# One core, retention then a gated FFN: the first blocks of w3 by rows instead of by columns, two weight casts exchanged, one product in other PSUM banks

## The chip, the cores and the metric

The kernel runs on one core of a Trainium2 chip. The metric is the device time of one execution in microseconds (us). Before the change it is 186.15 us, the median of 13 runs (185.81 to 189.73).

The engines are named as the profile names them: PE (TensorE: matmuls and transposes, with PEld its weight loads), DVE (VectorE), ACT (ScalarE), POOL (GpSimd) and SP (SyncE, which here issues nearly all DMAs). Each engine executes its own instructions strictly in the order in which they stand in the program; engines wait for each other and for DMAs by semaphores.

## What is computed

```
# retention, 4 batches x 8 heads x 768 steps x 64
state = gamma[h] * state + outer(k[t], v[t])
y[t]  = q[t] @ state / sqrt(64)
x = y, heads side by side                       # [3072, 512]
# gated FFN; w1, w2 [512, 1024], w3 [1024, 1024], w_out [1024, 512]
h   = ((x @ w1) * (x @ w2)) @ w3
out = h @ w_out
```

## The kernel before

Since nothing lies between `@ w3` and `@ w_out`, the kernel first forms the product W3O = w3 @ w_out (eight tiles of 128 x 512), and then needs only x @ w1, x @ w2, their product, and one matmul with W3O. Retention is done in chunks of 128 time steps. A step handles one chunk of two batches (256 tokens); there are 12 steps (`NSTEP`). All matmuls take 16-bit inputs, so each weight and each of q, k, v is loaded in 32 bits into a staging tile and cast by DVE, ACT or POOL.

The order of the instructions is written out by hand, so the order of the statements is the order on each engine.

**Loads.** All loads go through `dma_in` (L63) on SP's queue. At most eight are under way, since the ninth waits for the first to land, and so on. The first eight alternate: a quarter of the first half of w3 (`load_w3_columns`, four pieces of 1 KB per partition), then a quarter of w_out (`load_wo`, 4 KB per partition), four times. Then come the last four row blocks of w3 (`load_rows`, 4 KB per partition), q, k, v of the first two batches, w1, w2, and the data of the later steps.

**W3O, first half (row blocks f = 0 to 3).** w3 has to be transposed on PE before it can be the stationary operand. For each column quarter i the program casts it (`cast_w3`, on DVE), transposes it in 8 PE instructions (`w3_transpose_columns`), copies the result back (`w3_back`, L254, on DVE), casts the matching quarter of w_out (`cast_wo`, ACT and POOL), and adds 8 matmuls, two to each of four open accumulators (`w3_mm_columns`, L283). All four row blocks are complete only after the last quarter. `output_decays` (three DVE multiplications, L206, and three ACT exponentials, L210; a table of decay factors for later) stands between the first and the second quarter. `busy(8, n=208)`, eight matmuls of zeros whose result nobody reads, stands there too.

**W3O, second half (f = 4 to 7).** Here a whole row block is cast (on ACT), transposed in 8 instructions (`w3_transpose`), copied back, and multiplied by all of w_out in 8 matmuls (`w3_mm`, L296). The first chunk of attention (`b0`, `b1`: objects of class `Pairs`, batch 0 and batch 1) is woven into this: q and k casts, their transposes (L349), scores (L446), the product with v (L464), the states (L477, L488 to L494), and the state's contribution to the output (L501).

**Start of the FFN.** `by_rows` (L746) runs x @ w1, and later x @ w2, for step 0 one row block of the weight after another, as each arrives. Row block 1 of w1 is cast on POOL (L732); 0, 2 and 3 on ACT (`cast_w`, L226), in this order. On POOL the cast of batch 1's v (`b1.v_cast`, L432) and the second half of `b0.states()` (L494) stand ahead of it.

**Step 2.** `step2` runs the FFN of step 1 between the parts of attention step 2. `f1.ab(f)` takes one accumulator from the four rotating PSUM banks `psF`; DVE's multiplication L651 frees it. `kv(2)` (L551), the product of k and v, writes the two banks `X0` and `X1`, the same two that `scores` uses; `kv_back(0)` (L573) and `kv_back(1)` (L565) read them on DVE. Step 3 then begins with `inter(2)` (L599) and `scores(3)` (L400).

**Steps 5 to 12.** At the start of a step m the program calls `intra(m - 1)` (L531), then `inter(m - 1)` (L599), which adds to the same banks and waits for the former. The wait goes through a mark: a 1 x 1 copy on ACT (`ended`, L587). For the m in `EARLY = (6, 11)` `intra(m - 1)` is instead called in the middle of the step before, and there is no mark.

Of the kernel before, what the change touches and what calls it, by code (L numbers as in the profile page):

```python
# [10 lines left out]
HP = mybir.dt.float16  # L11
# [7 lines left out]
def kernel(  # L19
# [11 lines left out]
    nc = tc.nc  # L31
# [19 lines left out]
    att = ctx.enter_context(tc.tile_pool(name="att", bufs=2))  # L51
# [53 lines left out]
    def new_stage():  # L105
        return wstage.tile([128, 1024], FP, tag="wst", name="stg")

    def load_rows(src, i):
        t = new_stage()
        dma_in(t[:, :], src[i * 128 : (i + 1) * 128, :])  # L110
        return t

    def load_wo(i):
        t = new_stage()
        dma_in(
            t[:, :].rearrange("p (t n) -> p t n", t=2),
            moe_w_out[i * 256 : (i + 1) * 256, :].rearrange("(p t) n -> p t n", t=2),
        )
        return t

    def load_w3_columns(i):
        t = new_stage()
        dma_in(
            t[:, :].rearrange("p (f c) -> p f c", f=4),
            moe_w3[0:512, i * 256 : (i + 1) * 256].rearrange("(f p) c -> p f c", p=128),
        )
        return t

    w3c_st, wo_st = [], []
    for i in range(4):  # L130
        w3c_st.append(load_w3_columns(i))
        wo_st.append(load_wo(i))
    w3_st = {f: load_rows(moe_w3, f) for f in range(4, 8)}
    for e in range(2):
        load_q(e)
        k_in[e] = load_pairs(k, e, 0)
# [1 line left out]
    w1_st = [load_rows(moe_w1, d) for d in range(4)]  # L138
# [12 lines left out]
    ident16 = const.tile([128, 128], HP, name="ident16")  # L151
# [21 lines left out]
    for s in range(2):  # L173
        r = slice(s * L, (s + 1) * L)
# [24 lines left out]
    for h in range(H):  # L199
        p, r = h // 2, (h % 2) * 64  # L200
        nc.gpsimd.memset(GS[r : r + 64, p : p + 1], gam[h] ** C)

    def output_decays():
        for n, (s, swap) in enumerate(((0, 0), (1, 0), (1, 1))):
            x = fsb.tile([128, NP, L], FP, tag="pa", name="ys_x", bufs=8)
            nc.vector.tensor_tensor(  # L206
                x[:, :, :], if_f[:, s, :].unsqueeze(1).broadcast_to((128, NP, L)),
                LGP[:, swap, :].unsqueeze(2).broadcast_to((128, NP, L)), MULT,
            )
            nc.scalar.activation(YS[:, n, :, :], x[:, :, :], AF.Exp)  # L210
# [4 lines left out]
    W1 = [wpool.tile([128, DFF], HP, name=f"w1_{i}") for i in range(4)]  # L215
    W2 = [wpool.tile([128, DFF], HP, name=f"w2_{i}") for i in range(4)]
    WO = [wpool.tile([128, 2, DM], HP, name=f"wo_{i}") for i in range(4)]
    W3O = [wpool.tile([128, DM], HP, name=f"w3o_{i}") for i in range(8)]
    W3h = {}
    w3t = {}  # L220

    def cast_to(dst, src, on_dve):
        if on_dve:
            nc.vector.tensor_copy(dst, src)
        else:
            nc.scalar.copy(dst, src)  # L226

    def cast_wo(i):
        dst = WO[i][:, :, :].rearrange("p a n -> p (a n)")
        if i == 0:  # L230
            nc.scalar.copy(dst, wo_st[i][:, :])
        else:
            nc.scalar.copy(dst[:, 0:512], wo_st[i][:, 0:512])
            nc.gpsimd.tensor_copy(dst[:, 512:1024], wo_st[i][:, 512:1024])

    def cast_w3(key, st):
        t = att.tile([128, 1024], HP, tag="qT", name="w3h", bufs=5)
        if key == ("c", 0):
            nc.vector.tensor_copy(t[:, 0:512], st[:, 0:512])
            nc.scalar.copy(t[:, 512:1024], st[:, 512:1024])  # L240
        else:
            cast_to(t[:, :], st[:, :], key in (("c", 1), ("c", 2), ("c", 3)))
        W3h[key] = t

    def bank(tag, shape, dtype, name):
        return ps_at.tile(shape, dtype, tag=tag, name=name)

    def w3_bank(key, i):
        src = W3h.pop(key)
        return src, bank(("X0", "X1")[i % 2], [128, 1024], HP, "psW3")  # L250

    def w3_back(key, ps):
        t = att.tile([128, 1024], HP, tag="v16", name="w3t", bufs=3)
        nc.vector.tensor_copy(t[:, :], ps[:, :])  # L254
        w3t[key] = t

    def w3_transpose_columns(i):
        src, ps = w3_bank(("c", i), i)
        for f in range(4):
            for t in range(2):  # L260
                g, c0 = f * 2 + t, f * 256 + t
                nc.tensor.transpose(  # L262
                    ps[:, g * 128 : (g + 1) * 128], src[:, c0 : c0 + 255 : 2], ident16[:, :]
                )
        w3_back(("c", i), ps)

    def w3_transpose(f):
        src, ps = w3_bank(f, f)
        for g in range(8):
            c0 = (g // 2) * 256 + g % 2  # L270
            nc.tensor.transpose(
                ps[:, g * 128 : (g + 1) * 128], src[:, c0 : c0 + 255 : 2], ident16[:, :]
            )
        w3_back(f, ps)

    def w3_mm_columns(i, acc, between=None, at=3):
        t = w3t.pop(("c", i))
        for f in range(4):
            if f == at and between:
                between()  # L280
            for r in range(2):
                g = f * 2 + r
                nc.tensor.matmul(  # L283
                    acc[f], lhsT=t[:, g * 128 : (g + 1) * 128], rhs=WO[i][:, r, :],
                    start=(i == 0 and r == 0), stop=(i == 3 and r == 1),
                )
            if i == 3:
                cast_to(W3O[f][:, :], acc[f], f < 3)
# [125 lines left out]
    class Pairs:  # L414
# [261 lines left out]
    def busy(m, tag="Y0", n=512):  # L676
        if tag:
            ps = bank(tag, [128, 512], FP, "psZ")
        else:
            ps = ps_f.tile([128, 512], FP, tag="psF", name="psZ")  # L680
        for _ in range(m):
            nc.tensor.matmul(ps[:, 0:n], lhsT=Z[:, 0:128], rhs=Z[:, 0:n], start=True, stop=True)  # L682

    cast_w3(("c", 0), w3c_st[0])
    busy(8)
    acc = [ps_f.tile([128, DM], FP, tag="psF", name="psW")[:, :] for _ in range(4)]
    w3_transpose_columns(0)
    cast_wo(0)
    output_decays()
    busy(8, n=208)  # L690
    cast_w3(("c", 1), w3c_st[1])
    w3_mm_columns(0, acc)
    w3_transpose_columns(1)
    cast_wo(1)
    cast_w3(("c", 2), w3c_st[2])
    w3_mm_columns(1, acc, lambda: w3_transpose_columns(2))
    cast_wo(2)
    cast_w3(("c", 3), w3c_st[3])
    w3_mm_columns(2, acc, lambda: w3_transpose_columns(3))
    cast_wo(3)  # L700
    cast_w3(4, w3_st[4])
    cast_w3(5, w3_st[5])
    w3_mm_columns(3, acc)
    w3_transpose(4)
    w3_transpose(5)
    cast_w3(6, w3_st[6])
    cast_w3(7, w3_st[7])
# [15 lines left out]
    b0.intra()  # L723
    b0.kv()
    b0.outputs_back(0)
    b0.states()
    b1.v_cast((nc.gpsimd, nc.gpsimd))
    b1.k_transposes(None, False)
    b0.inter()
    b0.outputs_back(1)  # L730
    busy(1, None)
    nc.gpsimd.tensor_copy(W1[1][:, :], w1_st[1][:, :])  # L732
    for d in (0, 2, 3):
        cast_w(W1, w1_st, d, False)

    ffn = [Ffn(m) for m in range(NSTEP)]
# [16 lines left out]
    ps = four_banks()  # L753
# [25 lines left out]
    ps = four_banks()  # L779
# [24 lines left out]
    def step2():  # L804
        am_back = scores(2)
        am_back(0)
        am_back(1)
        f0.o_unit(1)
        k_cast(3, (nc.gpsimd, nc.scalar))
        for f in range(2, 5):  # L810
            f1.ab(f)
        intra(2)
        kv_back = kv(2)
        kv_back(0)
        f1.ab(5)
        f1.ab(6)
        k_transposes(3, None, (True, False))
        kv_back(1)
        v_cast(3, (nc.gpsimd, nc.gpsimd))
        f1.ab(7)  # L820

    EARLY = (6, 11)

    K_PE = (3, 6, 8)

    def step(m):

# [100 lines left out]
```

## Time and profile before

| what | value |
|---|---|
| median of 13 runs | 186.15 us |
| the profiled execution | 187.42 us |
| its span in the profile | 185.8 us |
| PE busy | 174.7 us, 94% of the span |
| DVE, ACT, POOL busy | 108.9, 82.4, 59.1 us |
| PE busy from 0 to 38 us | 31.98 us |
| PE busy from 38 to 60 us | 21.49 us |
| DMA rate, slices from 0 to 18.6 us | 198, 361, 383, 405 GB/s |

The span is the time from the first to the last record of one profiled execution; 1.6 us of that execution lie around it. A timeline line has the start in us, the duration, the engine, the program's line, the operation, output and input tiles with shapes, the number of merged instructions, and in brackets how long the engine had been idle before and what ended that. An engine's busy share counts matmuls to their modelled ends. PE's idle time lies mostly in the first 40 us, where weights and the first data arrive.

### The profile page before, as it was taken

The page shows a single profiled execution, that of the slowest core. Times are in us where ns is not written, and L with a number is a line of the kernel's source. Part 1 is how long each engine was busy: PE and PEld are TensorE (multiplying, and loading weights), DVE is VectorE, ACT ScalarE, POOL GpSimd, SP SyncE. Part 2 cuts the span into 40 slices and gives each one's busy share as a digit, 9 for nine tenths or more (in the row PEclk, how much of TensorE's full clock was granted, in tenths as well). Part 3 has the DMA queues.
Part 4 walks back from the last instruction along what each step waited for, and adds up shares of the span by engine and source line. Part 5 has one row for each costly group of instructions (what it writes and reads, how often), then busy time and mean ns, then how long its engine had stood idle before and what let it go on. Part 6 is the DMA issues. An engine that isn't in the chain of part 4 may idle for free.

```text
span 185.8 us, 6230 instructions
## 1 busy us (share of the span) xinstructions
PE 174.7 (94%) x2642; PEld 124.8 (67%) x2642; DVE 108.9 (59%) x204; ACT 82.4 (44%) x166; POOL 59.1 (32%) x107
## 2 busy tenths in 40 slices
PE   7879899799999899999999999999999999999992
PEld 2434555488756487685876968859778587684871
DVE  1546557770749567848558584495685856845330
ACT  3524846556741332643445436354364442441531
POOL 7421143744543951533304425016251060000000
PEclk9999999999999999999999999999999999999999
DMA  5999999999899998999989989999999960200203
GB/s 198 361 383 405 301 278 341 407 374 232 185 218 273 210 185 214 255 261 218 189 199 257 255 170 156 249 253 264 166 130 216 206 137 4 113 0 14 102 0 113
DMA packets 80010, 39.44 MB, mean 212 GB/s; under 512 B 56304, under 2 KB 74992, under 8 KB 79984
## 3 DMA queue, kind: packets, MB, share of 16 engines
q1 hardware_dynamic: 79552, 38.54, 83.2%
q8 instruction: 20, 0.33, 0.8%
q10 hardware_dynamic: 432, 0.52, 0.8%
q14 instruction: 6, 0.05, 0.1%
HBM read 29.36 MB, written 6.29 MB: 192 GB/s over the span
## 4 chain that ended last, share of the span: by engine, by line
PE 75%; DMA 9%; SPq 6%; POOL 2%; issue 2%; ACT 2%; DVE 1%; ACTq 0%; POOLq 0%; DVEq 0%
PE psF L636 39%; PE psO L661 23%; SPq L63 6%; DMA stg<-in_moe_w_out_dram 5%; DMA stg<-in_k_dram 4%; PE psF L746 3%; PE psY L531 2%; PE psA L400 2%; PE psG L636 2%; PE psK L551 2%; PE psY L599 2%; POOL v L432 1%; PE psTk L375 1%; POOL k L311 1%; ACT qT L226 1%
## 5 line engine op out<-in xcount | busy, mean ns | idle before, releaser
L636 PE MATMUL psF<-xt,w 128*128 128x256 f16 x672 | 76.7, 273 | 0.0
L636 PEld LDWEIGHTS <-w 128*128 128x128 f16 x704 | 68.3, 98 | 10.4
L651 DVE TENSOR_TENSOR ht<-pa,psF 128x256 f16<-128x256 f32 x88 | 36.8, 420 | 39.4 <-PE psF L636 21.3
L661 PE MATMUL psO<-w3o,ht 128*128 128x512 f16 (+2 forms) x200 | 43.9, 371 | 0.8 <-issue 0.8
L645 ACT COPY pa<-psF 128x256 f32<-128x256 f32 x80 | 29.7, 372 | 33.4 <-PE psF L636 33.3
L661 PEld LDWEIGHTS <-ht 128*128 128x128 f16 x200 | 18.5, 98 | 20.7 <-issue 1.1
L665 ACT ACTIVATE osb<-psO 128x512 f32<-128x512 f32 (+2 forms) x25 | 14.5, 580 | 35.1 <-PE psO L661 35.1
L566 POOL TENSOR_TENSOR t<-s,GS 128x512 f16<-128x512 f32 x8 | 8.3, 1040 | 50.0 <-DVE s L565 50.0
L614 DVE TENSOR_TENSOR xt<-psY,YS 64x512 f16<-64x512 f32 (+1 forms) x29 | 21.0, 726 | 5.0 <-PE psY L599 4.7
L331 POOL TENSOR_TENSOR v<-stg,VS 128x512 f16<-128x512 f32 x20 | 20.5, 1042 | 6.4 <-DMA stg<-in_v_dram 6.3
L311 POOL CAST q<-stg 128x1024 f16<-128x1024 f32 x11 | 11.4, 1039 | 17.1 <-DMA stg<-in_q_dram 16.3
L407 DVE TENSOR_TENSOR am<-psA,keep 128x512 f16<-128x512 f32 x20 | 12.8, 682 | 1.7 <-PE psA L400 1.7
L746 PE MATMUL psF<-xt,w 128*128 128x256 f16 x64 | 8.4, 274 | 1.4 <-POOL w L732 1.1
L283 PE MATMUL psW<-wo,w3t 128*128 128x512 f16 x32 | 7.9, 380 | 1.6 <-DVE w3t L254 1.5
L254 DVE COPY w3t<-psW 128x1024 f16<-128x1024 f16 x8 | 5.5, 690 | 5.8 <-PE psW L262 3.2
L324 ACT CAST k<-stg 128x1024 f16<-128x1024 f32 (+1 forms) x9 | 8.5, 944 | 0.0
L296 PE MATMUL psW<-wo,w3t 128*128 128x512 f16 x32 | 8.1, 380 | 0.0
L746 PEld LDWEIGHTS <-w 128*128 128x128 f16 x64 | 5.8, 98 | 2.9 <-POOL w L732 1.3
L573 DVE TENSOR_TENSOR t<-psK,t 128x512 f16<-128x512 f32 x9 | 6.2, 689 | 0.6 <-PE psK L551 0.5
L283 PEld LDWEIGHTS <-w3t 128*128 128x128 f16 x32 | 2.7, 98 | 5.3 <-DVE w3t L254 3.0
L451 DVE TENSOR_TENSOR am<-psA,keep_t 128x512 f16<-128x512 f32 x8 | 5.2, 686 | 1.7 <-PE psA L446 1.7
L682 PE MATMUL psZ<-zeros 128*128 128x512 f16 (+1 forms) x17 | 4.9, 439 | 1.3 <-DVE zeros L150 1.3
(90 smaller groups left out, 149.2 us busy)
## 6 DMA issues: line engine op xcount, KB each, us to landing
stg<-in_moe_w_dram SPq DMA_DIRECT2D x16, 512.0 KB, 8.9
stg<-in_q_dram SPq DMA_DIRECT2D x12, 512.0 KB, 6.2
out_dram<-osb SPq DMA_DIRECT2D x22, 256.0 KB, 3.5
stg<-in_k_dram SPq DMA_DIRECT2D x20, 256.0 KB, 5.5
stg<-in_v_dram SPq DMA_DIRECT2D x20, 256.0 KB, 5.5
stg<-in_moe_w_out_dram SPq DMA_DIRECT2D x4, 512.0 KB, 8.6
stg<-in_k_dram SPq DMA_DIRECT2D x2, 512.0 KB, 9.3
stg<-in_v_dram SPq DMA_DIRECT2D x2, 512.0 KB, 8.2
```

The lines of the kernel that those rows point to most:

```text
L63: nc.sync.dma_start(dst, src)
L283: nc.tensor.matmul(acc[f], lhsT=t[:, g * 128 : (g + 1) * 128], rhs=WO[i][:, r, :], start=(i == 0 and r == 0), stop=(i == 3 and r == 1),)
L311: (nc.scalar.copy if eng is nc.scalar else eng.tensor_copy)(dst[:, :].rearrange("i (t h d) -> i h t d", t=2, d=D), src[:, :].rearrange("i ...
L331: eng.tensor_tensor(v16[:, e, :].rearrange("j (h d) -> j h d", d=D), v32[:, e, :].rearrange("j (h d) -> j h d", d=D), VS[:, 2, :].unsqueez ...
L407: nc.vector.tensor_tensor(am[:, r, :, :], ps[r][:, :, :], keep[:, :].unsqueeze(1).broadcast_to((128, NP * 2, L)), MULT,)
L614: nc.vector.tensor_tensor(XT[m][to, :, s, :].rearrange("p (a e) (i t) -> p a e t i", e=2, t=2), psYs[m][s][fr, :, :].rearrange("p (a e) (t ...
L636: nc.tensor.matmul(ps[:, :], lhsT=W[d][:, f * 128 : (f + 1) * 128], rhs=self.x(d), start=(d == 0), stop=(d == 3),)
L645: nc.scalar.copy(self.pa[f][:, :], ps[:, :])
L651: nc.vector.tensor_tensor(self.HT[:, f, :], self.pa.pop(f)[:, :], ps[:, :], MULT)
L661: nc.tensor.matmul(psO[:, :], lhsT=self.HT[:, f, e * 128 : (e + 1) * 128], rhs=W3O[f][:, cs], start=(f == 0), stop=(f == 7),)
L665: nc.scalar.activation(osb[:, cs], psO[:, :], AF.Copy, scale=final_scale)
L746: nc.tensor.matmul(ps[f // 2][:, f % 2, :], lhsT=W[d][:, f * 128 : (f + 1) * 128], rhs=f0.x(d), start=(d == 0 and f % 2 == 0), stop=(d == ...
```

## The change

Five edits.

1. The first four w3 loads take whole row blocks (f = 0 to 3), in turns with w_out as before; no load is made by columns.
2. Consequently W3O's first half is computed in another order: as each row block and each quarter of w_out arrives, the parts that have become possible are multiplied (`w3_part(f, *parts)`, two matmuls for each part). `busy(8, n=208)` comes before the first part, and `output_decays` comes after the second transpose instead of after the first. The tile `w3t` of f < 3 is taken from the buffers of `k16`.
3. `b1.v_cast` moves ahead of `b0.states()`, and POOL casts row block 2 of w1 where it cast row block 1; ACT casts 0, 1 and 3.
4. `kv(2)` writes two of the rotating `psF` banks instead of `X0` and `X1`.
5. `EARLY` becomes `(6, 11, 12)`.

The number of instructions on PE, DVE and POOL stays the same (matmuls, transposes, casts); ACT has one less, a mark.

```diff
-    w3c_st, wo_st = [], []
+    w3_st, wo_st = [], []
     for i in range(4):
-        w3c_st.append(load_w3_columns(i))
+        w3_st.append(load_rows(moe_w3, i))
         wo_st.append(load_wo(i))
-    w3_st = {f: load_rows(moe_w3, f) for f in range(4, 8)}
+    for f in range(4, 8):
+        w3_st.append(load_rows(moe_w3, f))
...
+        w3t[f] = att.tile([128, 1024], HP, tag="k16" if f < 3 else "v16", name="w3t", bufs=3)
+        nc.vector.tensor_copy(w3t[f][:, :], ps[:, :])
+
+    def w3_part(f, *parts):
+        for i in parts:
             for r in range(2):
-                g = f * 2 + r
+                g = i * 2 + r
                 nc.tensor.matmul(
-                    acc[f], lhsT=t[:, g * 128 : (g + 1) * 128], rhs=WO[i][:, r, :],
-                    start=(i == 0 and r == 0), stop=(i == 3 and r == 1),
+                    acc[f], lhsT=w3t[f][:, g * 128 : (g + 1) * 128], rhs=WO[i][:, r, :],
+                    start=(g == 0), stop=(g == 7),
                 )
             if i == 3:
                 cast_to(W3O[f][:, :], acc[f], f < 3)
...
-    cast_w3(("c", 0), w3c_st[0])
+    cast_w3(0)
     busy(8)
     acc = [ps_f.tile([128, DM], FP, tag="psF", name="psW")[:, :] for _ in range(4)]
-    w3_transpose_columns(0)
+    w3_transpose(0)
     cast_wo(0)
+    busy(8, n=208)
+    w3_part(0, 0)
+    cast_w3(1)
+    w3_transpose(1)
     output_decays()
-    busy(8, n=208)
-    cast_w3(("c", 1), w3c_st[1])
-    w3_mm_columns(0, acc)
-    w3_transpose_columns(1)
     cast_wo(1)
-    cast_w3(("c", 2), w3c_st[2])
-    w3_mm_columns(1, acc, lambda: w3_transpose_columns(2))
+    w3_part(0, 1)
+    w3_part(1, 0, 1)
+    cast_w3(2)
+    w3_transpose(2)
     cast_wo(2)
-    cast_w3(("c", 3), w3c_st[3])
-    w3_mm_columns(2, acc, lambda: w3_transpose_columns(3))
+    w3_part(0, 2)
+    w3_part(1, 2)
+    w3_part(2, 0)
+    cast_w3(3)
+    w3_transpose(3)
+    w3_part(2, 1, 2)
     cast_wo(3)
-    cast_w3(4, w3_st[4])
-    cast_w3(5, w3_st[5])
-    w3_mm_columns(3, acc)
+    cast_w3(4)
+    cast_w3(5)
+    for f in range(3):
+        w3_part(f, 3)
+    w3_part(3, 0, 1)
     w3_transpose(4)
+    w3_part(3, 2, 3)
     w3_transpose(5)
...
     b0.outputs_back(0)
+    b1.v_cast((nc.gpsimd, nc.gpsimd))
     b0.states()
-    b1.v_cast((nc.gpsimd, nc.gpsimd))
...
-    nc.gpsimd.tensor_copy(W1[1][:, :], w1_st[1][:, :])
-    for d in (0, 2, 3):
+    nc.gpsimd.tensor_copy(W1[2][:, :], w1_st[2][:, :])
+    for d in (0, 1, 3):
         cast_w(W1, w1_st, d, False)
...
-        kv_back = kv(2)
+        kv_back = kv(2, True)
...
-    EARLY = (6, 11)
+    EARLY = (6, 11, 12)
```

More of the change, by code (lines that the diff above doesn't have):

```diff
@@ L119, in load_wo @@
         return t
[L121 to L127, printed above, removed]
-    w3c_st, wo_st = [], []
+    w3_st, wo_st = [], []
     for i in range(4):
-        w3c_st.append(load_w3_columns(i))
+        w3_st.append(load_rows(moe_w3, i))
         wo_st.append(load_wo(i))
-    w3_st = {f: load_rows(moe_w3, f) for f in range(4, 8)}
+    for f in range(4, 8):
+        w3_st.append(load_rows(moe_w3, f))
     for e in range(2):
@@ L234, in cast_wo, with cast_w3 @@
             nc.gpsimd.tensor_copy(dst[:, 512:1024], wo_st[i][:, 512:1024])
-    def cast_w3(key, st):
+    def cast_w3(f):
         t = att.tile([128, 1024], HP, tag="qT", name="w3h", bufs=5)
-        if key == ("c", 0):
+        st = w3_st[f]
+        if f == 0:
             nc.vector.tensor_copy(t[:, 0:512], st[:, 0:512])
@@ L241, in cast_w3 @@
         else:
-            cast_to(t[:, :], st[:, :], key in (("c", 1), ("c", 2), ("c", 3)))
-        W3h[key] = t
+            cast_to(t[:, :], st[:, :], f < 4)
+        W3h[f] = t
     def bank(tag, shape, dtype, name):
         return ps_at.tile(shape, dtype, tag=tag, name=name)
[L248 to L265, printed above, removed]
     def w3_transpose(f):
-        src, ps = w3_bank(f, f)
+        src, ps = W3h.pop(f), bank(("X0", "X1")[f % 2], [128, 1024], HP, "psW3")
         for g in range(8):
@@ L273, in w3_transpose @@
             )
[L274 to L280, printed above, removed]
+        w3t[f] = att.tile([128, 1024], HP, tag="k16" if f < 3 else "v16", name="w3t", bufs=3)
+        nc.vector.tensor_copy(w3t[f][:, :], ps[:, :])
+    def w3_part(f, *parts):
+        for i in parts:
             for r in range(2):
-                g = f * 2 + r
+                g = i * 2 + r
                 nc.tensor.matmul(
-                    acc[f], lhsT=t[:, g * 128 : (g + 1) * 128], rhs=WO[i][:, r, :],
-                    start=(i == 0 and r == 0), stop=(i == 3 and r == 1),
+                    acc[f], lhsT=w3t[f][:, g * 128 : (g + 1) * 128], rhs=WO[i][:, r, :],
+                    start=(g == 0), stop=(g == 7),
                 )
@@ L682, in busy @@
             nc.tensor.matmul(ps[:, 0:n], lhsT=Z[:, 0:128], rhs=Z[:, 0:n], start=True, stop=True)
-    cast_w3(("c", 0), w3c_st[0])
+    cast_w3(0)
     busy(8)
     acc = [ps_f.tile([128, DM], FP, tag="psF", name="psW")[:, :] for _ in range(4)]
-    w3_transpose_columns(0)
+    w3_transpose(0)
     cast_wo(0)
+    busy(8, n=208)
+    w3_part(0, 0)
+    cast_w3(1)
+    w3_transpose(1)
     output_decays()
-    busy(8, n=208)
-    cast_w3(("c", 1), w3c_st[1])
-    w3_mm_columns(0, acc)
-    w3_transpose_columns(1)
     cast_wo(1)
-    cast_w3(("c", 2), w3c_st[2])
-    w3_mm_columns(1, acc, lambda: w3_transpose_columns(2))
+    w3_part(0, 1)
+    w3_part(1, 0, 1)
+    cast_w3(2)
+    w3_transpose(2)
     cast_wo(2)
-    cast_w3(("c", 3), w3c_st[3])
-    w3_mm_columns(2, acc, lambda: w3_transpose_columns(3))
-    cast_wo(3)
-    cast_w3(4, w3_st[4])
-    cast_w3(5, w3_st[5])
-    w3_mm_columns(3, acc)
+    w3_part(0, 2)
[4 more added lines that the diff above has]
+    w3_part(2, 1, 2)
+    cast_wo(3)
+    cast_w3(4)
[3 more added lines that the diff above has]
+    w3_part(3, 0, 1)
     w3_transpose(4)
+    w3_part(3, 2, 3)
     w3_transpose(5)
-    cast_w3(6, w3_st[6])
-    cast_w3(7, w3_st[7])
+    cast_w3(6)
+    cast_w3(7)
     w3_mm(4, lambda: w3_transpose(6))()
```

## The prediction, made before the changed kernel ran

> **What bounds the kernel now.** First the page: the busy shares and the chain of work that ended last.
>
> ```profile
> PE 174.7 (94%) x2642; PEld 124.8 (67%) x2642; DVE 108.9 (59%) x204; ACT 82.4 (44%) x166; POOL 59.1 (32%) x107
> ...
> PE 75%; DMA 9%; SPq 6%; POOL 2%; issue 2%; ACT 2%; DVE 1%; ACTq 0%; POOLq 0%; DVEq 0%
> ```
>
> PE bounds the kernel, and its instructions stay the same in number and shape. So the change is worth what it does to PE's waits: before 40 us, in step 2 (56 to 63 us), and at step 12. I take the timeline at these places. First the start:
>
> ```profile
> 6.72 1.08 DVE L206 TENSOR_TENSOR ys_x<-if_f,LGP 128x256 f32<-128x256 f32 x3
> ...
> 7.17 1.08 ACT L210 ACTIVATE YS<-ys_x 128x256 f32<-128x256 f32 x3 [0.34 <-DVE ys_x L206]
> 8.73 0.69 DVE L224 CAST w3h<-stg 128x1024 f16<-128x1024 f32 x1 [0.93 <-DMA stg<-in_moe_w_dram]
> ...
> 10.03 0.62 ACT L233 CAST wo<-stg 128x512 f16<-128x512 f32 x1 [1.77 <-DMA stg<-in_moe_w_out_dram]
> ...
> 10.89 1.47 PE L283 MATMUL psW<-wo,w3t 128*128 128x512 f16 x6 [0.79 <-DVE w3t L254]
> ...
> 14.32 0.69 DVE L224 CAST w3h<-stg 128x1024 f16<-128x1024 f32 x1 [0.69 <-DMA stg<-in_moe_w_dram]
> ...
> 15.60 0.62 ACT L233 CAST wo<-stg 128x512 f16<-128x512 f32 x1 [2.16 <-DMA stg<-in_moe_w_out_dram]
> ...
> 24.25 0.61 PE L349 MATMUL psTq<-ident,q 128*128 128x128 f16 x8
> ```
>
> The decays (L206, L210) lie in a gap in which DVE and ACT wait for DMA anyway (0.93 and 1.77 us of idle are left behind them). The eight matmuls of the first quarter (6.88 to 8.6) lie before it too. From 20.75 to 31.8 PE hardly waits: what delays it at 24.25 delays everything up to batch 1's scores. The landings show the DMA: a column load after a w_out load costs 1.50 us (12.82 to 14.32), a row-wise one after a column load 1.28 (14.32 to 15.60).
>
> **Edits 1 and 2, the start.** I follow the chain through the new order. *Landings.* Four column loads become row loads, each 1.50 − 1.28 = 0.22 us quicker. The first cast starts at 4.27 instead of 4.47, that of the second w3 block (two such loads) at 8.33 instead of 8.73. Bounds: 8.73, if pieces of 1 KB cost nothing, and 6.9 (4.27 and two row loads of 1.3) if the odd step of 2.95 us from 5.78 to 8.73 were due to columns; it looks like a start-up lag, so I take 8.33.
>
> *The new wait.* DVE casts (0.69), PE transposes (0.62), DVE copies back (0.69), with 0.05 us between each: to 10.43. Now come the three decays on DVE, 1.08, and behind them ACT's three exponentials, which end 0.45 after the last decay (8.25 against 7.80 before): 11.96. In ACT's queue the cast of the second w_out quarter stands behind them; its data has long landed (9.6). It ends at 12.6, and PE's next product (part 0,1) starts at 12.66. Before, this matmul group started at 10.89, and eight matmuls of the group before it were done, where now there are two. Queued on PE behind it are all parts of blocks 0 to 3.
>
> *From there to the first q transpose* PE has 46 matmuls of 128x512 (30 for blocks 0 to 3, 16 for blocks 4 and 5) at 0.216 (1.90 for eight, less the 0.17 tail) and six sets of transposes at 0.45: 9.94 + 2.70 = 12.64. Waits in between: 0.10 for the copy-back of block 2; 0.26 for block 3's cast, which DVE can begin only after that copy; 0.6 for block 6's cast, as ACT first has to evict block 3 (L226, 0.58), whose last part now ends at 21.0, after the transposes of block 4. Sum 12.66 + 13.6 = 26.26, against 24.25: **+2.0 us**. With the landing at 8.73 it is +2.4.
>
> [...]
>
> **Edit 3, w1's casts.**
>
> ```profile
> 35.27 1.03 POOL L732 CAST w<-stg 128x1024 f16<-128x1024 f32 x1
> ...
> 36.37 1.05 PE L746 MATMUL psF<-xt,w 128*128 128x256 f16 x8 [1.11 <-POOL w L732]
> ```
>
> POOL casts w1's block 1 only after the v cast (33.28, 2.05 us), which stood behind L494, which waits for DVE (2.03 us): PE waits 1.11. After: batch 1's data land by about 31 us, so v is cast before L494; ACT casts blocks 0 and 1 back to back behind kT. With +2.0, block 0's matmuls start at 35.84, ACT has block 1 at 36.9, the second scores run at 36.82, and block 1's matmuls start at 37.1, not at 38.4. Then DVE's masking of these scores (1.29 for two halves from 37.27) ends at 38.56 and takes the wait's place: the second half of intra starts at 38.62, `kv` and then block 2's matmuls at 39.24, against 38.20. Left: **+1.04**, so this edit gives back 0.96. Block 2's cast on POOL (free at 35.3) ends at 36.4, block 3's on ACT at 37.95: both hidden. From here to 56 us the waits are on work of PE's own chain (data for step 2 land 1 to 3 us early), so +1.04 stays.
>
> **Edit 4, kv(2) in psF.**
>
> ```profile
> 58.79 0.44 PE L400 MATMUL psA<-qT,kT 64*64 64x64 f16 x30 [0.28 <-DVE s L565]
> ...
> 62.96 0.81 PE L661 MATMUL psO<-w3o,ht 128*128 128x512 f16 x3 [0.82 <-issue]
> ```
>
> The scores of step 3 no longer wait for `kv_back(1)` (0.28). But counting the rotation, `f1.ab(7)` gets the bank that `kv` filled second, and waits for the same `kv_back(1)`, ending at 58.73. Its four matmuls (0.45) and `inter(2)` (0.37), which ran before that point, now run after it: 0.82, plus 0.02 for the start. The outputs then begin 0.84 later than the 59.16 of before. Cover: the 0.82 us in which PE stood still before 62.96, a wait that no engine's record explains ("issue"). If its end is tied to a moment in PE's stream ahead of the edit, it swallows 0.82 of the 0.84; if to the position alone, nothing. Ends 0.02 and 0.84; I take **0.02**, since nothing in the queues of the other engines holds these three matmuls, so it seems to be a supply of instructions running alongside.
>
> **Edit 5.**
>
> ```profile
> 167.68 0.19 ACT L587 COPY mark<-zeros 1x1 f16<-1x1 f16 x1 [0.47 <-PE psY L531]
> ...
> 167.93 0.45 PE L599 MATMUL psY<-qT,t 64*64 64x64 f16 x32 [0.31 <-ACT mark L587]
> ```
>
> Intra (0.38) moves to 161.8 in step 11; the masked scores are ready at 160.87 and Y's banks at 158.95. The 0.31 us of waiting goes: **−0.30**.
>
> **Sum** against the profiled execution: A +2.0, B −0.96, C +0.02, D −0.30 = +0.76; span 185.8 → 186.55, the execution 187.42 → 188.2. That execution is 1.27 above the median, so against the median 186.15: **186.9 us**.
>
> **Rivals.**
> *PE falls back to half rate.* Eight 128x512 matmuls took 3.60 us at 1.26 and 1.90 at 16.48. After the change PE does next to nothing from 7.3 to 12.66, two sets of transposes apart at most. If it slows, one more such stretch costs 1.70, nothing gives it back, and the time is 188.6. Against it: after the idle stretch 8.61 to 10.89, with transposes in it, matmuls ran at full rate; but now it is 5.4 us. The granted clock reads 1.00 throughout, even at 1.26, so the clock column won't tell; durations will.
> [...]
> *Edit 4's wait isn't covered:* +0.82, 187.7. For it: the stall's cause isn't shown.
> *Faster: the load lag belongs to the column loads.* If the second w3 block is cast at 6.9 instead of 8.33, the whole chain to 24.25 moves with it by 1.43: the sum becomes 0.76 − 1.43 = −0.67, 185.5. The sum passes nought at a cast at 7.57, and the difference can be measured from 7.0 on. Against it: at 5.7 us 1.3 MB had moved, at 8.7 us 2.4 MB, while the landed loads are 1.05 and 1.57; the DMAs worked without a gap, part of them ran ahead, and the slowest one sets the landing, whatever the shape.
> *The rows land early but nothing follows*, as PE was never waiting: the landings alone are then hidden, and the time stays at 186.1 to 186.4. This needs the decays off the chain, which the order of ACT's queue excludes; small.
>
> **Chances.** Forecast (186.4 to 187.4) 0.40; uncovered wait 0.20; half rate 0.18; faster 0.15; flat 0.07. Range 185.6 to 188.7. A measurement tells 0.3%, 0.56 us, from no change: faster is below 185.6, slower above 186.7. The forecast's own spread puts a third of it below 186.7: slower 0.27 + 0.20 + 0.18 = 0.65; same 0.13 + 0.07 + some of the faster case = 0.22; faster 0.13.
>
> **What would show it.** ACT's cast of the second w_out quarter starts near 12.0 behind L210's line, with no DMA wait; the first q transpose at 26.3; by_rows block 1 without a POOL wait and block 2 about 1 us later than 38.20; `f1.ab(7)` waiting for DVE's `s`, and no 0.82 us standstill in step 3's outputs; no mark at step 12. I am wrong if the second w3 cast starts before 7.6, if matmuls after 12.66 take 0.43 us each, or if a standstill appears elsewhere.

## The result, and the profile after

The changed kernel takes 188.33 us, the median of 11 runs (187.62 to 189.25). The kernel before has a median of 186.41 us (48 runs). The ratio is 1.0102, with a 95% interval of 1.0078 to 1.0126: the change makes the kernel 1% slower. All ratios leave out the runs that are over 1.5% above the fastest of the same kernel. The profiled execution took 188.88 us, its span 186.8, so 2.08 us lie around the span where 1.62 did before.

The page of the changed kernel: busy time by engine, the granted clock in 40 slices of 4.67 us (in tenths), and the chain that ended last.

```profile
PE 176.6 (95%) x2642; PEld 126.4 (68%) x2642; DVE 108.6 (58%) x204; ACT 81.7 (44%) x165; POOL 59.1 (32%) x107
...
PEclk9957999999999999999999999999999999999999
...
PE 75%; ACT 2%; DVE 1%; issue 0%; ACTq 0%; DVEq 0%
```

PE does the same 2642 operations but is "busy" 1.9 us longer. The clock row says where: slices 3 and 4, from 9.3 to 18.7 us. The windows of the changed kernel give the same by stage (stretch, its length, PE's busy time, granted clock, DMA share, GB/s):

```profile
9.00:14.00 5.00, 2.26 (x13) 0.58 1.02 416
14.00:18.60 4.60, 4.60 (x29) 0.71 1.04 392
18.60:23.30 4.70, 4.70 (x36) 1.00 1.16 292
```

Finer windows of the same trace show 1.00 from 6 to 9.80 us, 0.50 from 9.80 to 16.63, and 1.00 behind it: 6.83 us at half rate.

The timeline of the changed kernel at the start, in the columns used before:

```profile
8.15 0.69 DVE L217 CAST w3h<-stg 128x1024 f16<-128x1024 f32 x1 [1.63 <-DMA stg<-in_moe_w_dram]
...
10.61 1.09 ACT L203 ACTIVATE YS<-ys_x 128x256 f32<-128x256 f32 x3 [4.12 <-DVE ys_x L199]
...
11.61 1.12 ACT L226 CAST wo<-stg 128x512 f16<-128x512 f32 x2
...
12.26 2.72 PE L257 MATMUL psW<-wo,w3t 128*128 128x512 f16 x6 [2.74 <-ACT wo L226]
...
14.77 1.06 PE L246 MATMUL psW<-ident,w3h 128*128 128x128 f16 x8
...
27.48 0.61 PE L323 MATMUL psTq<-ident,q 128*128 128x128 f16 x8
```

ACT waits 4.12 us for DVE's decays. Its cast of the second w_out quarter stands behind the exponentials and has no DMA wait any more, and PE waits for that cast. Six products then take 2.72 us (1.47 before), and eight transposes 1.06 instead of 0.62: half rate.

Later places in the changed kernel's timeline: `by_rows` blocks 0, 1 and 2; step 2's `f1.ab(7)`, the second half of step 3's scores and its outputs; intra in step 11, and inter of step 12:

```profile
37.07 1.05 PE L729 MATMUL psF<-xt,w 128*128 128x256 f16 x8 [0.21 <-ACT w L219]
...
38.42 1.05 PE L729 MATMUL psF<-xt,w 128*128 128x256 f16 x8
...
40.44 1.05 PE L729 MATMUL psF<-xt,w 128*128 128x256 f16 x8
...
59.81 0.60 PE L610 MATMUL psF<-xt,w 128*128 128x256 f16 x4
...
61.16 0.32 PE L374 MATMUL psA<-qT,kT 64*64 64x64 f16 x16 [0.25 <-ACT kT L219]
61.41 3.63 PE L635 MATMUL psO<-w3o,ht 128*128 128x512 f16 x16
...
163.36 0.44 PE L505 MATMUL psY<-am,v 64*64 64x64 f16 x32
...
169.08 0.45 PE L573 MATMUL psY<-qT,t 64*64 64x64 f16 x32
```

Two of these places in the kernel before, `by_rows` block 2 and the outputs of step 3:

```profile
38.20 1.05 PE L746 MATMUL psF<-xt,w 128*128 128x256 f16 x8
...
59.16 2.98 PE L661 MATMUL psO<-w3o,ht 128*128 128x512 f16 x13
```

Block 1 no longer waits for POOL, step 3's scores wait 0.25 for kT on ACT where they waited 0.28 for DVE's `s`, step 3's 16 outputs run without a standstill (a stop of PE in the middle of a group, with nothing in the profile that it waits for), and step 12 has no mark. How far the changed kernel is behind at each place:

| place | before | after | behind |
|---|---|---|---|
| product after the second w_out cast | 10.89 | 12.26 | 1.37 |
| first q transpose | 24.25 | 27.48 | 3.23 |
| `by_rows` block 2 | 38.20 | 40.44 | 2.24 |
| outputs of step 3 | 59.16 | 61.41 | 2.25 |
| the FFN products behind them | 63.61 | 64.88 | 1.27 |
| outputs behind step 12's start | 168.30 | 169.46 | 1.16 |
| span | 185.8 | 186.8 | 1.0 |

The start costs 3.23, edit 3 gives back 0.99, edit 4 nothing (0.01). A standstill of the kernel before, which the changed kernel doesn't have in this execution, gives 0.98. Between 64.88 and step 12 the gap rises to 1.43, and edit 5 gives back 0.27.

### The profile page after: what moved, and what is told of

It reads as the page before. It is cut to its first block, busy times and chain, and to the rows that moved or that the text cites. A ratio compares the mean times of both kernels' runs of the same rounds, so it can differ in the third digit from the quotient of the medians.

```text
span 186.8 us, 6225 instructions
## 1 busy us (share of the span) xinstructions
PE 176.6 (95%) x2642; PEld 126.4 (68%) x2642; DVE 108.6 (58%) x204; ACT 81.7 (44%) x165; POOL 59.1 (32%) x107
## 4 chain that ended last, share of the span: by engine, by line
PE 75%; ACT 2%; DVE 1%; issue 0%; ACTq 0%; DVEq 0%
PE psF L610 38%; PE psO L635 22%; PE psF L729 4%; PE psY L505 2%; PE psA L374 2%; PE psG L610 2%; PE psY L573 2%; PE psK L525 2%; PE psTk L349 1%; ACT qT L219 1%; ACT w L219 1%; ACT osb L639 0%; PE psY L438 0%; DVE ht L625 0%; ACT kT L219 0%
## 5 line engine op out<-in xcount | busy, mean ns | idle before, releaser
L257 PE MATMUL psW<-wo,w3t 128*128 128x512 f16 x32 | 9.5, 444 | 2.7 <-ACT wo L226 2.7
L246 PEld LDWEIGHTS <-w3h 128*128 128x128 f16 x64 | 4.7, 109 | 5.2 <-DVE w3h L217 2.1
L270 PE MATMUL psW<-wo,w3t 128*128 128x512 f16 x32 | 8.1, 380 | 0.0
L257 PEld LDWEIGHTS <-w3t 128*128 128x128 f16 x32 | 3.4, 110 | 6.4 <-issue 4.5
L246 PE MATMUL psW<-ident,w3h 128*128 128x128 f16 x64 | 5.8, 243 | 1.9 <-DVE w3h L217 1.6
L219 ACT CAST w3o<-psW 128x512 f16<-128x512 f32 x5 | 2.9, 585 | 8.7 <-PE psW L270 4.6
```

The source lines that it names most:

```text
L246: nc.tensor.transpose(ps[:, g * 128 : (g + 1) * 128], src[:, c0 : c0 + 255 : 2], ident16[:, :])
L257: nc.tensor.matmul(acc[f], lhsT=w3t[f][:, g * 128 : (g + 1) * 128], rhs=WO[i][:, r, :], start=(g == 0), stop=(g == 7),)
```

## The experiments

Each kernel was timed beside the kernel before on the same chip. Four questions are asked: what the decays' place and the clock each cost; what edits 3 to 5 give; what the standstill is; and why 0.45 us more lie outside the span.

**The kernel before, again** (`e1_before_again`), with no edit.

> The kernel before, unchanged, so that its spread and its standstill at 62 us can be seen in a second profile. If the 0.82 us standstill in the outputs of step 3 belongs to a place in PE's stream, it is there again, with about the same length; if it depends on how other traffic happens to fall, it may be gone, and the span then is near 185.0 instead of 185.8. Time 186.1 to 186.5.

Measured: 186.06 us median, spans 184.2 to 185.1. Its profiled execution has no standstill; the 16 outputs of step 3 and the FFN products behind them:

```profile
59.30 3.63 PE L661 MATMUL psO<-w3o,ht 128*128 128x512 f16 x16
62.76 1.91 PE L636 MATMUL psF<-xt,w 128*128 128x256 f16 x16
```

From the first output to the FFN products it is 3.46 us here and was 4.45 in the profiled execution before. The standstill (0.99 with its surroundings) is in one of the two profiles of the unchanged kernel and not in the other.

**The decays back at their old place** (`e2_decays_early`):

```diff
     cast_wo(0)
+    output_decays()
     busy(8, n=208)
...
     w3_transpose(1)
-    output_decays()
```

> The changed kernel, but output_decays stands again right behind the cast of the first w_out quarter. My theory (the late decays hold ACT's cast of the second w_out quarter, and the idle stretch that follows halves PE's rate): that cast starts near 9.6 with no wait for the exponentials, part (0,1) starts near 10.3 instead of 12.26, the matmuls take 0.216 and not 0.43, the first q transpose falls back from 27.5 to 24.2-24.6, and the time is 185.0 to 186.0, below both kernels. Rival (the order by rows is itself what costs, since ten matmuls instead of eight are left after the last w_out quarter, and a block's eviction stands before the casts of blocks 6 and 7 on ACT): the first q transpose gains under 1.5 us and the time stays above 187.

Measured: 185.81 us (185.42 to 186.55), ratio 0.9959 [0.9932, 0.9986]: the whole loss is gone. Its timeline:

```profile
9.52 0.62 ACT L226 CAST wo<-stg 128x512 f16<-128x512 f32 x1 [1.63 <-DMA stg<-in_moe_w_out_dram]
...
10.19 2.35 PE L257 MATMUL psW<-wo,w3t 128*128 128x512 f16 x6 [0.56 <-ACT wo L226]
...
24.95 0.61 PE L323 MATMUL psTq<-ident,q 128*128 128x128 f16 x8
```

ACT's cast waits for its DMA again, and PE has it two us sooner. The six products still run mostly at half rate here (2.35). In five of the ten runs the mean clock was 0.988 to 0.991 and the span 183.8 to 184.5; in the other five 0.997 to 1.0 and 183.4 to 183.6. So the order by rows, with two products ahead of the gap where the order by columns has eight, costs something of its own: with the decays early and the second w3 cast at the same time (8.26 and 8.28), the order by columns further down (`e5_rows_only`) has its first q transpose at 23.39, this run at 24.95.

**Only the decays moved, in the kernel before** (`e6_cols_late_decays`):

```diff
     cast_wo(0)
-    output_decays()
...
     w3_transpose_columns(1)
+    output_decays()
     cast_wo(1)
```

> The kernel before, with column loads and its own order, in which only the three decays move behind the transposes of the second w3 load, ahead of the second w_out cast: the place that the change gives them. Theory (the place of the decays alone makes the late start): ACT's second w_out cast at about 12.4 instead of 10.03, the next product at about 13.0 instead of 10.89; 24 matmuls and two sets of transposes from there bring the last product of the first four blocks to 17.8 instead of 16.48, so the first q transpose is at 25.5 if PE stays at full rate, at 26.8 to 27.3 if the matmuls after 13.0 take 0.43 us each; span +1.3 to +2.9. Rival (the order by rows makes it, not the decays): the first q transpose stays within 0.3 of 24.3.

Measured: 188.69 us (4 runs), ratio 1.0134 [1.0102, 1.0166]. With column loads and the old order, one moved call makes the same picture:

```profile
11.38 1.12 ACT L233 CAST wo<-stg 128x512 f16<-128x512 f32 x2
...
12.03 1.48 PE L283 MATMUL psW<-wo,w3t 128*128 128x512 f16 x6 [2.74 <-ACT wo L233]
13.32 1.04 PE L262 MATMUL psW<-ident,w3h 128*128 128x128 f16 x8
...
14.16 3.23 PE L283 MATMUL psW<-wo,w3t 128*128 128x512 f16 x8
...
26.16 0.61 PE L349 MATMUL psTq<-ident,q 128*128 128x128 f16 x8
```

The first q transpose is 1.9 later than before, between the two numbers expected, although the second w3 cast came 1.43 earlier here (7.30). The first six products are at full rate and the next eight, after transposes, are at half: the mean granted clock is 0.93 from 9.3 to 14 us and 0.70 from 14 to 18.6; at 0.50 that puts its fall at 13.3 us, when the six have run, and its return at 16.8 (an estimate). The rival (the row order makes the loss) falls as the main cause; its smaller share is named above.

**Filler in the gap** (`e3_warm`): eleven products of zeros ahead of the decays, so that PE isn't idle.

```diff
     w3_transpose(1)
+    busy(11)
     output_decays()
```

> The changed kernel with eleven matmuls of zeros (128x512) behind the second w3 transposes, inside the time in which PE waits for the second w_out quarter; the wait itself stays. It parts the two halves of the loss. If half rate is an effect of the idle stretch, the matmuls from 12.3 on take 0.216 each, the first q transpose falls from 27.5 to 26.1-26.4, the mean granted clock is 0.99 or more and the time is 187.0 to 187.6. If the low rate has another cause, matmuls still take 0.43 and the time stays at 188.3.

Measured: 190.7 us, four runs from 187.76 to 192.07, ratio (of the two shorter ones) 1.012 [0.9985, 1.0256], unclear, and not the 187.0 to 187.6 expected. Two of the four still had a mean clock of 0.989 and 0.990. The profiled run had 0.998, and its trace is clearer than its time; the first products behind the gap, the first q transpose, and two places in the outputs:

```profile
11.86 1.46 PE L257 MATMUL psW<-wo,w3t 128*128 128x512 f16 x6 [0.37 <-ACT wo L226]
...
25.48 0.61 PE L323 MATMUL psTq<-ident,q 128*128 128x128 f16 x8
...
61.85 3.18 PE L635 MATMUL psO<-w3o,ht 128*128 128x512 f16 x14 [1.84 <-issue]
...
137.89 1.46 PE L635 MATMUL psO<-w3o,ht 128*128 128x512 f16 x6 [1.39 <-issue]
```

The six products run at full rate, 1.46 us. From them to the first q transpose (25.48) it is 13.62 us, against 15.22 in the changed kernel: the half clock costs the profiled execution of the changed kernel 1.60. In six of that kernel's twelve runs the mean clock is 0.981 or 0.982 as there (spans 186.7 to 187.2), in the other six 0.989 to 0.991 (185.5 to 186.2); these lost some 1.1 us less. What the filler gave was lost again to two standstills. In the kernel before 3 of the 16 outputs were left at the standstill, here 14: eleven products more have been put ahead, and the standstill has moved eleven products forward in the outputs. Counted in PE's program, weight loads and products each as one, both stand at number 1472, and the second at 4032, 2560 further. So in these two profiles the place belongs to a position in PE's program and not to the work done there.

**Edits 1 and 2 alone** (`e8_start_only`): the changed kernel, with `v_cast`, the casts of w1, `kv(2)` and `EARLY` as before.

> The changed kernel with edits 3, 4 and 5 undone: edits 1 and 2 alone. Theory (the start costs all of it, the other edits give back 1.3): second w_out cast on ACT at 11.6, matmuls from 12.2 at 0.43 us each, first q transpose at 27.5, block 2 of by_rows at 41.3 to 41.6, span 187.7 to 188.4, time ratio 1.015 to 1.022. Rival (edit 4 costs something that the trace of the changed kernel hides): span below 187.5, ratio about 1.010.

Measured: 189.2 us (4 runs), ratio 1.0173 [1.0138, 1.0208]; the six products start at 11.66, the first q transpose at 26.43, as the second w3 cast came at 7.55 here. At a clock of 0.989 to 0.991 its spans are 186.8 to 187.2, those of the changed kernel 185.5 to 186.2: edits 3 to 5 give back some 1.1 us of the 1.26 read from the profiles. The span is below 187.5, as the rival had it, but from the early cast. Edit 4 hides no cost: from `by_rows` block 2 to the outputs of step 3 it is 20.96 us here without the edit, 20.97 in the changed kernel with it.

**Edits 3 to 5, and 3 and 5, in the kernel before** (`e4_before_345`, `e7_before_35`):

```diff
+    b1.v_cast((nc.gpsimd, nc.gpsimd))
     b0.states()
-    b1.v_cast((nc.gpsimd, nc.gpsimd))
...
-    nc.gpsimd.tensor_copy(W1[1][:, :], w1_st[1][:, :])
-    for d in (0, 2, 3):
+    nc.gpsimd.tensor_copy(W1[2][:, :], w1_st[2][:, :])
+    for d in (0, 1, 3):
...
-        kv_back = kv(2)
+        kv_back = kv(2, True)
...
-    EARLY = (6, 11)
+    EARLY = (6, 11, 12)
```

The line of `kv(2)` is changed in the first of the two only.

> The kernel before with only edits 3, 4 and 5: w1's casts exchanged with v ahead of the states, kv(2) in psF, EARLY with 12. By my steps edit 3 gives 0.9 to 1.0 where block 1 of w1 is waited for, edit 4 nothing (the profile after shows the scores of step 3 now waiting for kT on ACT by 0.25 instead of for s by 0.28), edit 5 0.3: together 1.2, so 184.9 to 185.2. Rival: w1's block 1 has not landed when ACT gets to it (it lands near 33.8 here), or the standstill of step 3 grows by what was gained ahead of it, as it shrank by 0.98 when PE came 2.2 us late; then the gain is 0.3 to 0.5, 185.7 to 186.1.

> The kernel before with edit 3 (the v cast ahead of L494, the casts of w1's blocks 1 and 2 exchanged) and edit 5 (an early intra at step 12), without the rest. Theory: block 1 of by_rows without a wait for POOL, block 2 at 37.1 to 37.3 instead of 38.2, no mark at step 12; span 1.25 to 1.3 shorter than the kernel before in runs without a standstill (182.8 to 183.8), time ratio 0.993. Rival (the standstills in PE's stream take the gain up): time ratio 0.997 to 1.0.

Measured: 186.5 us, ratio 0.9972 [0.9932, 1.0012], and 186.49 us, ratio 1.0004 [0.9975, 1.0032]. No gain that can be told from nothing, with spans from 183.4 to 186.3 and from 183.5 to 186.1. From block 2 to the outputs of step 3 it is 20.96 us with edit 4 and 20.97 without, 20.96 in the kernel before: edit 4 is worth nothing here either. The shortest spans are 0.5 to 0.7 below the shortest of the kernel before in the same sets of runs (184.0 and 184.1), not 1.25. The profile of the run with 3 and 5 shows one way in which the gain goes (cast of w1's block 0, then blocks 0 and 1 of `by_rows`):

```profile
33.94 1.04 ACT L226 CAST w<-stg 128x1024 f16<-128x1024 f32 x1 [0.70 <-DMA stg<-in_moe_w_dram]
...
35.04 1.57 PE L746 MATMUL psF<-xt,w 128*128 128x256 f16 x8 [1.01 <-DVE am L451]
...
37.14 1.85 PE L746 MATMUL psF<-xt,w 128*128 128x256 f16 x8
```

The first block of w1 landed at least 1.2 us later than in the profile before (cast at 32.74 there, without a DMA wait). PE waited 1.01 for it (the masking named as the releaser ends at about the same moment as the cast; in the kernel before, the block starts in the middle of it), and then the clock fell (0.80 from 33 to 37 us, 0.77 from 37 to 41): 1.57 and 1.85 us for eight products that otherwise take 1.05.

**Only the loads by rows** (`e5_rows_only`), with the order of the columns kept; the first four blocks of W3O are then made of other pieces.

```diff
-        w3c_st.append(load_w3_columns(i))
+        w3c_st.append(load_rows(moe_w3, i))
```

> The kernel before, in which only the first four loads of w3 fetch whole rows (blocks 0 to 3) instead of column strips; the order of the products stays that of the columns, so the first four blocks of W3O are made of the wrong pieces. Theory (the DMA side of edit 1 is a gain of 0.2 us per load): the second w3 cast starts at 8.2 to 8.4 instead of 8.73, the fourth one 0.8 us earlier than 14.32, the first q transpose at 23.5 to 23.7 instead of 24.25 to 24.39; span 183.3 to 184.3 without a standstill. Rival (the landings are set by bytes alone): casts and the first q transpose where they were, span 184.1 to 185. On the 0.45 us by which the changed kernel's time exceeds its span more than before: if the row loads cause it, time less span is about 2.05 here, otherwise 1.6 to 1.7.

Measured: 185.31 us, ratio 0.9974 [0.9946, 1.0002]. The second w3 cast comes at 8.28, the next ones at 10.87 and 13.43. That is 2.57 us for a pair of loads, where the run with edits 3 and 5 has 2.79 (8.64, 11.43, 14.22): 0.22 for each row load. The first q transpose is at 23.39. But block 0 of `by_rows` is no earlier (33.84 in the kernel before):

```profile
23.39 0.61 PE L349 MATMUL psTq<-ident,q 128*128 128x128 f16 x8
...
32.86 1.04 ACT L226 CAST w<-stg 128x1024 f16<-128x1024 f32 x1 [0.87 <-DMA stg<-in_moe_w_dram]
33.96 1.84 PE L746 MATMUL psF<-xt,w 128*128 128x256 f16 x8 [1.18 <-ACT w L226]
```

PE arrives early, waits 1.18 us for w1, and its clock falls at the end of this wait (0.63 from 33 to 37 us, which at 0.50 puts the fall at 34.0, an estimate; eight products take 1.84). In the nine runs at a clock of 0.998 or more the span is 183.1 to 185.6, in the one at 0.988 it is 185.2.

**Early decays, with block 3 of W3O evicted by DVE** (`e9_early_evict_dve`), on top of the run with the decays at their old place:

```diff
-                cast_to(W3O[f][:, :], acc[f], f < 3)
+                cast_to(W3O[f][:, :], acc[f], True)
```

> The changed kernel with the decays early (as in the run with the decays at their old place) and block 3 of W3O evicted by DVE instead of ACT, so that ACT's casts of blocks 6 and 7 don't stand behind it. Theory (the eviction in ACT's queue costs the 0.31 us at the transposes of block 6): that wait is gone, the first q transpose at 24.3 to 24.7 instead of 24.95, block 0 of by_rows up to 0.3 earlier than 34.55, span 183.1 to 183.7, time 185.3 to 185.7. Rival (DVE has no room: its eviction holds the copy-back of block 5): the first q transpose at 25.0 or later, time 185.8 or more.

Measured: 185.5 us (184.38 to 186.36), ratio 0.9939 [0.9909, 0.9969], the lowest ratio of the study, ahead of both kernels. The first q transpose is at 24.05, block 0 of `by_rows` at 33.75 and block 1 at 35.68; the cast ahead of the latter, at 34.58, waits 0.89 us for its DMA. It is ahead of the profile without this edit by 0.90 at the q transpose, 0.80 at block 0, 0.22 at block 1 and 0.41 at block 2: from here the loads of w1 bound it. Of the 0.90, 0.41 are there before block 3 is evicted (transposes of block 5 at 19.26 against 19.67: the second w3 cast came at 8.10 instead of 8.26, and the clock was back sooner: the eight transposes at 12.47 took 0.61 here, those at 12.32 without this edit 1.06), and 0.49 come with the wait at block 6's transposes. The spans, 182.6 to 184.6, are no shorter than without the edit (183.4 to 184.5); the 0.3 us between the medians (185.81 and 185.5) go with the time outside the span, 1.66 to 1.78 here and 2.02 to 2.12 there, to which the last two experiments come.

**Early decays and four fillers** (`e11_early_warm`):

```diff
     w3_part(0, 0)
+    busy(4)
     cast_w3(1)
```

> The changed kernel with the decays early and four filler products of 128x512 behind the first two parts, in PE's gap before the second w3 cast. Theory (the clock is halved because PE does nothing but transposes from 7.3 to 10.2): no run with a mean clock below 0.996 from this stretch, the six matmuls after 10.1 take 1.46 us instead of 2.35, the first q transpose at 24.0 to 24.3, span 183.0 to 183.5 in runs without a standstill, time 185.1 to 185.6. Rival (the loads of w1 bound block 0 of by_rows anyway, and the wait there halves the clock later): the first q transpose as early, but block 0 at 33.9 or later behind a DMA wait, and some runs at a clock of 0.988 to 0.991; time as with the decays early, 185.8.

Measured: 186.14 us, ratio 0.998 [0.995, 1.0009]. The lowest clock of the twelve runs is 0.997, where five of ten were at 0.988 to 0.991 without the fillers, and the six products take 1.57: here products in the gap held the clock. The first q transpose is at 22.99, 1.96 earlier than without the fillers, but 0.90 of that is the second w3 cast, at 7.36 here. Block 0 of `by_rows` is at 33.03, behind a cast that waited for its DMA until 31.93. The four shortest spans are 183.1 to 183.5, as expected; the other eight are 183.8 to 187.2 at the same clock. Whether these are standstills isn't shown, as the profiled run was one of the short ones.

**The pool slots alone** (`e10_tags`): the run with the row loads alone, with the slots of `k16` for the first three transposed blocks.

```diff
-        t = att.tile([128, 1024], HP, tag="v16", name="w3t", bufs=3)
+        t = att.tile([128, 1024], HP, tag="k16" if key in (("c", 0), ("c", 1), ("c", 2)) else "v16", name="w3t", bufs=3)
```

> The kernel before with the first four w3 loads by rows (the first four blocks of W3O are made of the wrong pieces), in which the first three transposed blocks also take the pool slots of k16, as in the change. It is for the 0.45 us by which time exceeds span in every kernel with edits 1 and 2. If the slots are its cause: time less span 2.05 to 2.1. If the row-wise order of the products is (the one part left): 1.6 to 1.7. Nothing else should move against the run with the row loads alone: span 183.1 to 184 without a standstill.

Measured: 186.26 us, ratio 0.9992 [0.9961, 1.0024], spans 183.6 to 185.1; time less span 2.04 to 2.11 in all eight runs, where the run with the row loads alone has 1.59 to 1.67. So the slots bring the 0.45. But the run with the eviction on DVE has the slots too, and 1.66 to 1.78. What goes with the numbers in all twelve kernels so far is the length of DVE's program, waits included: 322, 320 or 319 instructions (other slots need three waits less). With 322 it is 1.57 to 1.72, with 320 1.66 to 1.78, with 319 2.02 to 2.17, apart from two runs of the kernel with eleven fillers (2.67 and 2.74).

**Three idle DVE instructions more, in the changed kernel** (`e12_dve_three_more`):

```diff
+    spare = const.tile([1, 4], FP, name="spare")
+    for j in range(3):
+        nc.vector.memset(spare[:, j : j + 1], 0.0)
     ident16 = const.tile([128, 128], HP, name="ident16")
```

> The changed kernel with three idle DVE instructions more (memsets of one element each, read by nobody, in a stretch in which DVE waits for GpSimd). It is for the time outside the span. In the kernels run so far that time goes with the length of DVE's program, waits on semaphores counted: 1.6 to 1.7 us at 322 instructions (before and all kernels with its DVE program), 1.66 to 1.78 at 320 (the run with the eviction on DVE), 2.02 to 2.15 at 319 (every other kernel with the changed slots, the run with the slots alone among them). Theory (the length of DVE's program sets it): with 322 again, time less span 1.6 to 1.7, span unchanged (185.6 to 187.2), median 187.7 to 188.1. Rival (the slots themselves, or what DVE waits for, set it): 2.02 to 2.15, median 188.3.

Measured: 188.12 us, ratio 1.0072 [1.0037, 1.0107]; time less span 1.60 to 1.70 in all ten runs. At the same span of 186.8 the time is 188.40 to 188.45 (188.88 and 188.91 in the changed kernel). Three instructions of no use make the program 0.45 us shorter outside the span. The rival falls; why the length matters isn't shown.

## Why the prediction failed in part

The direction was right, the time was not: 186.9 was forecast, with a range of its own up to 187.4, and 188.33 came. It lies in the outer range because a rival happened, and close to that rival's 188.6 in part by luck: the wait was 0.4 smaller than worked out, and 0.45 outside the span was in no step.

*Edits 1 and 2, the new wait: right in mechanism.* ACT's second w_out cast behind the exponentials, without a DMA wait, and PE behind it, as written. From the w3 cast to PE's product it was 4.11 us (8.15 to 12.26), worked out as 4.33; the cast came at 8.15 against 8.33. From there 13.6 was worked out, and with the fillers that held the clock 13.62 was measured. Without the clock, A would have been 12.26 + 13.6 − 24.25 = +1.6, not +2.0. Moving the decays alone shows the cause (ratio 1.0134), moving them back shows it the other way (0.9959).

*PE falls back to half rate: this step decided, and I had it as a rival at 0.18.* By the prediction's own sign (matmuls behind the wait at 0.43 us each) it was wrong here: six took 2.72. The argument against the rival was wrong. I took the stretch from 8.61 to 10.89, after which products ran at full rate, as evidence; the kernel before gets through 2.3 us, the changed one not through 5.0 (7.3 to 12.3), in which the clock fell at 9.80. The price (1.70; 1.60 measured) was right in part by luck: it was meant for eight products at half rate, 3.60 us, and the profiled execution had 6.83 us of it, of which 9.80 to 12.26 fell into the wait. I also wrote that the clock column wouldn't tell: it reads 0.58 and 0.71. It is silent only at the very start, where eight products took 3.60 us at a reading of 1.00. Transposes in the gap didn't keep the clock: eight ran at 8.90 us, and it fell at 9.80. At 0.50 the trace's stretch of 6.83 us takes 3.4 of 186.8 us, 0.018, off the mean clock, and the mean of this execution is 0.982. The run with the decays early reads 0.64 from 9.3 to 14 us, the row loads alone read 0.63 from 33 to 37 and 0.94 from 37 to 41, edits 3 and 5 alone 0.80 and 0.77 there: at 0.50 each comes to 3.4 us (an estimate), half of 6.83 and 0.009 of a span. The changed kernel's twelve runs lie near one such stretch, at 0.989 to 0.991, or near two, at 0.981 to 0.982.

*Edit 3: right.* −0.96 worked out, −0.99 measured. Masking of the second scores took the wait's place as described. What I didn't see is that the gain holds only while PE is late: without the late start, blocks of w1 land too late for it (block 0 cast at 33.94 behind a DMA wait in one profile, at 32.74 without one before).

*Edit 4: wrong in the working, right in the number by chance.* The rotation was miscounted: `f1.ab(7)` starts at 59.81, ahead of DVE's `s` at 60.35, and has no idle time, so it doesn't wait for it. No 0.84 had to be covered, and nothing covered it. The standstill of 0.82 wasn't swallowed either; it belongs to PE's program at number 1472 and is there in some executions and not in others, with edit 4 (the run with the filler) and without it (the kernel before).

*Edit 5: right.* −0.30 worked out, −0.27 measured.

*The sum.* It was +0.76 against the profiled execution; +1.0 came in the span and +0.45 outside it. The span's +1.0 contains −0.98 of a standstill that only the profiled execution before had. Against an undisturbed execution before (184.9 in the second profile) the loss of span is 1.9 us: +1.6 the wait, +1.6 the clock, −0.99, −0.27. The 0.45 outside the span was in no step at all. Nothing in the profile's rows could have given it.

*The rival "the load lag belongs to the column loads"* falls: in the profiles the second w3 cast is at 7.30 to 8.73 with column loads (five profiles) and at 7.36 to 8.28 with row loads (nine). That landing varies by a microsecond between executions, whatever the shape; the 0.22 for each row load shows only in the pairs behind it.

## What to carry to other kernels

When a chain of small work is moved on two engines, look at what stands behind its last instruction in the slower engine's queue, and at how long the bound engine then does nothing that holds its clock: here, in the profiled execution, the wait cost 1.6 us and the clock the same again. A stage that gains time ahead of a load that is already just in time gives it back there, in two profiles with a drop of the clock on top (to 0.63 and 0.80 from 33 to 37 us). Before a difference of a few tenths is put down to an edit, see whether a standstill or the time outside the span has changed.

## What the runs showed of the hardware

- In the changed kernel the clock halved in a gap in which PE had nothing but transposes: at 9.80 us, 2.5 us into the gap from 7.3 to 12.3, and it stayed at 0.50 for 6.83 us. With products of zeros in the gap the profiled run had a mean clock of 0.998 (eleven; two of that kernel's four runs still had 0.989 and 0.990) and the lowest of twelve runs 0.997 (four, with the decays early). In two profiles the clock fell behind a wait of 1.18 and 1.01 us that ended at 33.96 and 35.04 (mean 0.63 and 0.80 from 33 to 37). Which executions it strikes differs (five of ten with the decays early).
- PE's standstills without a releaser, 0.82, 1.84 and 1.39 us, stand at two positions of its program (number 1472 in two kernels, and 4032, which is 2560 further) and come and go: the first profile of the kernel before has one, its second profile and the changed kernel's have none, the run with eleven fillers has two. What PE waits for there isn't shown; the supply of instructions that the prediction took for it was my estimate, and no run varied it (a DMA queue named "instruction" moved 0.33 MB in 20 packets in the profile before and in the one after alike).
- The time outside the span went from 2.05–2.13 (changed kernel, twelve runs) to 1.60–1.70 us (ten runs) when DVE's program grew from 319 to 322 instructions.
